# Loading wk and wv as joint 2560-byte rows, taking block 0 four tokens to a partition, and weaving k of the first tiles between the weight folds

## The chip, the cores and the metric

One core of one Trainium2 chip. The time is the device time of one execution in microseconds (us), the median of the undisturbed ("fast") executions. A profile is one execution on the chip; its span is about 1.9 us shorter than the time of the same execution (304.7 against 306.63 us for the kernel before). Times are compared inside the same rounds on the same chip, because the kernel before itself had medians from 306.7 to 307.4 us on different sets of rounds.

## The reference

```python
def A(x, wqkv, w_phi, wo):                      # S = 2048, D = 640, H = 32 heads of Dh = 20
    q, k, v = split(x @ wqkv)
    pq, pk = einsum("hsd,hdf->hsf", q, w_phi), einsum("hsd,hdf->hsf", k, w_phi)
    phi = lambda p: concat([softmax(p, -1), softmax(-p, -1)], -1)
    kv, z = einsum("hsf,hsd->hfd", phi(pk), v), phi(pk).sum(over s)
    o = einsum("hqf,hfd->hqd", phi(pq), kv) / (einsum("hqf,hf->hq", phi(pq), z) + 1e-6)
    return o @ wo
def B(x, w_gate, w_up, w_down):                 # F = 1728
    return (gelu(x @ w_gate) * (x @ w_up)) @ w_down
g = sigmoid((x * gate_w).sum(-1))
out = g * A(x) + (1 - g) * B(x)                 # all in bf16
```

## The kernel before

The 2048 tokens are 16 tiles of 128. Before the steady state, the kernel has a start-up of some 28 us, and only that is touched here:

1. `xtok` (the first four tiles of x) is transposed by TensorE (PE), two tiles copied by ScalarE (ACT), two by VectorE (DVE).
2. v of the four tiles is computed, contraction slab by slab, as the slabs of wv arrive.
3. wk is transposed by PE (six head groups) and multiplied by a block-diagonal matrix of w_phi: the "fold". The five folded slabs `wk2` give k already mapped through w_phi. The same is done with wq, whose transposes come from six transposing loads (`wqT`).
4. k of the tiles 0 to 3, exp of k on ACT (`Ek`), then the q projections (`pq`), and from there on a stream of v/k, q and Gram products (`gram`: v times the normalised exps of k; `k_norm`: DVE normalises them).

`self.ps`, the memory that PE writes its products to, is divided by this program into eight banks of 512 columns. A product that overwrites a bank has to wait until ACT or DVE has read out what stood there.

```python
# loads (order of issue)
xload(0, "sp"); xload(2, "act"); xload(1, "sp"); xload(3, "act")     # 160 KB each, rows of 1280 bytes
for kt in range(KD):                                                  # five slabs of wv, 160 KB each
    sc.dma("sp", ... self.wvk[:, kt, 0:D] <- w3[:, kt, 2 * D:3 * D], writes=[("wv", kt)])
sc.dma("act", ... wphi_sb <- w_phi)                                   # rows of 40 bytes
sc.dma("sp", ... self.wk_raw <- w3[:, :, D:2 * D], writes=["wk_raw"]) # 800 KB
sc.dma("sp", gload, writes=["wgate"])                                 # gate_w as a column, 2-byte elements
for g in range(6):                                                    # six transposing loads of wq
    sc.dma("sp", ... dma_start_transpose(self.wqT[:, g, :], ...), reads=["wk_raw"] if g == 0 else [])
... three transposing loads of x (tiles 4 to 15), then all FFN weights ...

# attention_state, start-up
for i in range(NWARM): matmul on zeros into bank 3                    # 7, warm-up
for t, ek in enumerate("adad"): self.x_transpose(t, 4 + t, ek)
self.v_first({... wk transposes of two groups inside the last slab ...})
self.w_transposes("k", (2, 3, 4, 5), (0, 6, 7, 0), "dadd")
...
for kt, (bk, ek) in enumerate(zip((6, 1, 4, 6, 0), "adada")):         # a: copied by ACT, d: by DVE
    self.fold(kt, "k", (bk, bk + 1), ek)
self.k_early(0, 2)            # k of tile 0 in the PSUM banks 2, 3; then its exp on ACT
self.k_early(1, 4)
self.fold(0, "q", (6, 7), "d")
self.fold(1, "q", (0, 1), "a")
self.k_early(2, 2)
self.fold(2, "q", (6, 7), "d")
self.fold(3, "q", (0, 1), "a")
self.fold(4, "q", (6, 7), "d")
self.k_norm(0)
self.k_early(3, 4)
self.k_norm(1)
self.pq(0, 1, 1); self.pq(0, 0, 0); self.pq(0, 3, 3)
self.gram(0)
self.k_norm(2)
self.pq(0, 2, 2)
...
```

The softmax here doesn't subtract the row's maximum and nothing guards it: scores larger than these inputs give would overflow.

## Time and profile before

| | before |
|---|---|
| time, median of the first 4 executions | 306.72 us (306.5 to 307.06) |
| span of the profile | 304.7 us |
| PE busy | 298.0 us |
| first v product / first q projection / third q projection | 6.93 / 25.46 / 28.12 us |

The page of the kernel before, its first and its busy line, and the first line of the chain that ended last:

```profile
span 304.7 us, 5022 instructions
PE 298.0 (98%) x2011; PEld 175.3 (58%) x2011; DVE 160.0 (53%) x312; ACT 106.8 (35%) x189; POOL 29.8 (10%) x59
PE 94%; DMA 2%; ACT 1%; DVE 1%; issue 0%; SPq 0%; ACTq 0%; DVEq 0%
```

PE is the bottleneck over the whole span. What is left to win is the time in which PE stands still. The table of stretches of the kernel before shows where most of that is (columns: stretch in us from the span's start and its length, then busy us of PE, weight loads, DVE, ACT, POOL with instruction counts, PE's granted clock, DMA share, GB/s):

```profile
4.00:8.00 4.00, 3.38 (x30) 2.58 (x28) 0.98 (x2) 1.41 (x2) 3.13 (x21) 1.00 1.01 302
...
16.00:20.00 4.00, 3.51 (x36) 2.31 (x34) 1.65 (x2) 2.65 (x6) 0.00 (x0) 1.00 0.69 129
20.00:24.00 4.00, 3.32 (x44) 2.71 (x42) 1.65 (x2) 3.99 (x10) 0.00 (x0) 1.00 0.91 190
24.00:28.00 4.00, 3.79 (x26) 1.95 (x23) 3.56 (x5) 2.85 (x7) 0.00 (x0) 1.00 1.11 224
```

0.62 us are lost from 4 to 8 us, 0.49 from 16 to 20, 0.68 from 20 to 24, 0.21 from 24 to 28. The view of waits, for PE alone, names what ended each idle time (total us, times, longest; left out are the wait for the first operand, at 1.26 us, and a later one of 0.2 us):

```profile
PE ps L345 <- DVE wq_50 L358: 0.7, 1, 0.7
PE ps L376 <- DMA wvk<-in_A_wqkv_dram: 0.6, 1, 0.6
PE ps L488 <- ACT Eq L494: 0.3, 1, 0.3
PE ps L345 <- ACT wvk L360: 0.3, 1, 0.3
PE ps L365 <- DVE wvk L358: 0.2, 1, 0.2
```

L376 is v, L345 the folds, L365 k, L488 the q projections. The timeline of the kernel before (start us, duration us, engine, line, out<-in, count, idle time before and what ended it) has the steps:

```profile
6.93 2.34 PE L376 MATMUL ps<-wvk,xT 128*128 128x480 bf16 x16 [0.62 <-DMA wvk<-in_A_wqkv_dram]
...
10.63 8.33 SPq L227 DMA_TRANSPOSE wqT<-in_A_wqkv_dram  x6
...
19.29 1.30 ACT L423 ACTIVATE Ek<-ps 128x640 bf16<-128x640 f32 x2 [1.04 <-PE ps L365]
...
20.39 0.77 PE L345 MATMUL ps<-BD,wqT 120*128 120x120 bf16 x12
...
21.00 1.53 PE L365 MATMUL ps<-wvk,xT 128*128 128x384 bf16 x10
...
25.46 2.32 PE L488 MATMUL ps<-xT,wq_50 128*128 128x512 bf16 x10
```

They are: v; the issue of the six wq transposes, which waits for wk; exp of k of tile 0; the first wq folds; k of tile 2 ("third k"); the first two q projections. Two marks are read from the chain of waits of the kernel before: the last product of the first wk fold, which waits for a copy of the transposed wk (the piece of the chain that starts there takes in three products of the next fold), and the third q projection, behind which PE never waits again for more than 0.2 us:

```profile
15.53 0.37 PE ps L345 x4
...
28.12 1.25 PE ps L488 x5
```

### The profile page before, as it was taken

The page shows a single profiled execution, that of the slowest core. Times are in us where ns is not written, and L with a number is a line of the kernel's source. Part 1 is how long each engine was busy: PE and PEld are TensorE (multiplying, and loading weights), DVE is VectorE, ACT ScalarE, POOL GpSimd, SP SyncE. Part 2 cuts the span into 40 slices and gives each one's busy share as a digit, 9 for nine tenths or more (in the row PEclk, how much of TensorE's full clock was granted, in tenths as well). Part 3 has the DMA queues.
Part 4 walks back from the last instruction along what each step waited for, and adds up shares of the span by engine and source line. Part 5 has one row for each costly group of instructions (what it writes and reads, how often), then busy time and mean ns, then how long its engine had stood idle before and what let it go on. Part 6 is the DMA issues. An engine that isn't in the chain of part 4 may idle for free.

```text
span 304.7 us, 5022 instructions
## 1 busy us (share of the span) xinstructions
PE 298.0 (98%) x2011; PEld 175.3 (58%) x2011; DVE 160.0 (53%) x312; ACT 106.8 (35%) x189; POOL 29.8 (10%) x59
## 2 busy tenths in 40 slices
PE   7998999999999999999999999999999999999996
PEld 4664565655555555677545567754457764545763
DVE  1438999586775877234367710435770044567000
ACT  3388666667674222111322211123221122222111
POOL 7100000000000011111011000101110010111000
PEclk9999999999999999999999999999999999999999
DMA  7589996000000011120120111011111001110401
GB/s 222 140 150 209 369 369 221 0 2 0 2 0 0 2 22 24 24 65 25 43 20 4 22 24 43 24 43 23 17 6 44 24 26 41 22 22 0 45 22 45
DMA packets 34641, 18.29 MB, mean 60 GB/s; under 512 B 25850, under 2 KB 34618, under 8 KB 34618
## 3 DMA queue, kind: packets, MB, share of 16 engines
q1 hardware_dynamic: 33680, 17.62, 22.8%
q10 hardware_dynamic: 938, 0.35, 0.4%
q8 instruction: 16, 0.26, 0.4%
q14 instruction: 7, 0.06, 0.1%
HBM read 9.78 MB, written 2.62 MB: 41 GB/s over the span
## 4 chain that ended last, share of the span: by engine, by line
PE 94%; DMA 2%; ACT 1%; DVE 1%; issue 0%; SPq 0%; ACTq 0%; DVEq 0%
PE ps L572 37%; PE ps L654 20%; PE ps L365 12%; PE ps L660 7%; PE ps L488 6%; PE ps L609 4%; PE ps L462 4%; PE ps L376 2%; DMA wvk<-in_A_wqkv_dram 2%; PE ps L582 1%; PE ps L345 1%; ACT Eq L494 1%; PE ps L327 0%; ACT Ek L423 0%; DVE wkT L334 0%
## 5 line engine op out<-in xcount | busy, mean ns | idle before, releaser
L572 PE MATMUL ps<-xT,wu_sb 128*128 128x512 bf16 x260 | 64.6, 379 | 0.2 <-ACT Eq L494 0.2
L572 PE MATMUL ps<-xT,wg_sb 128*128 128x512 bf16 x260 | 64.6, 379 | 0.0
L654 PE MATMUL ps<-wd_sb,hT 128*128 128x320 bf16 (+2 forms) x448 | 63.8, 299 | 0.0
L575 ACT ACTIVATE gl<-ps 128x512 bf16<-128x512 f32 x52 | 31.1, 597 | 83.2 <-PE ps L572 81.0
L577 DVE TENSOR_TENSOR hT<-ps,gl 128x512 bf16<-128x512 f32 x52 | 35.7, 688 | 42.9 <-PE ps L572 42.9
L654 PEld LDWEIGHTS ps<-wd_sb,hT 128*128 128x128 bf16 x448 | 43.1, 98 | 18.2 <-DVE hT L577 0.4
L572 PEld LDWEIGHTS ps<-xT,wu_sb 128*128 128x128 bf16 x260 | 25.4, 98 | 31.1 <-issue 0.7
L365 PE MATMUL ps<-wvk,xT 128*128 128x512 bf16 (+2 forms) x220 | 40.6, 335 | 0.2 <-DVE wvk L358 0.2
L572 PEld LDWEIGHTS ps<-xT,wg_sb 128*128 128x128 bf16 x260 | 24.9, 98 | 26.9
L670 ACT ACTIVATE outsb<-ps,Gm 128x640 bf16<-128x640 f32 (+2 forms) x17 | 13.0, 763 | 74.1 <-PE ps L660 74.1
L638 POOL TENSOR_TENSOR Og<-O_59,O_60 128x640 bf16<-128x640 bf16 x16 | 22.3, 1396 | 167.8 <-DVE O_60 L636 167.8
L365 PEld LDWEIGHTS ps<-wvk,xT 128*128 128x128 bf16 x220 | 21.1, 97 | 19.5 <-DVE wvk L358 0.6
L434 DVE TENSOR_REDUCE Dk<-Ek 128x64 f32<-128x1280 bf16 x16 | 23.7, 1482 | 10.0 <-ACT gcol L426 10.0
L625 DVE RECIPROCAL RH<-ps 128x32 f32<-128x32 f32 x16 | 5.7, 358 | 43.9 <-PE ps L609 42.8
L443 DVE TENSOR_TENSOR Ek<-Ek,Dk 128x640 bf16<-128x640 bf16 x32 | 25.0, 822 | 0.5
L488 PE MATMUL ps<-xT,wq_50 128*128 128x512 bf16 x100 | 24.7, 378 | 0.3 <-ACT Eq L494 0.3
L660 PE MATMUL ps<-wo_sb,goT 128*128 128x320 bf16 (+2 forms) x160 | 24.5, 299 | 0.0
L494 ACT ACTIVATE Eq<-ps 128x512 bf16<-128x512 f32 x40 | 21.8, 607 | 5.4 <-PE ps L488 5.4
L423 ACT ACTIVATE Ek<-ps 128x640 bf16<-128x640 f32 x32 | 20.7, 703 | 2.2 <-PE ps L365 2.2
L660 PEld LDWEIGHTS ps<-wo_sb,goT 128*128 128x128 bf16 x160 | 15.5, 98 | 6.3
L609 PEld LDWEIGHTS ps<-KV,Eq 128*128 128x128 bf16 x192 | 12.0, 98 | 3.1
L609 PE MATMUL ps<-KV,Eq 128*128 128x154 bf16 x192 | 13.7, 221 | 0.0
(68 smaller groups left out, 178.7 us busy)
## 6 DMA issues: line engine op xcount, KB each, us to landing
out_dram<-outsb SPq DMA_DIRECT2D x15, 160.0 KB, 1.8
wd_sb<-in_B_w_down_dram SPq DMA_DIRECT2D x1, 2080.0 KB, 12.7
wg_sb<-in_B_w_gate_dram SPq DMA_DIRECT2D x1, 1120.0 KB, 7.0
wu_sb<-in_B_w_up_dram SPq DMA_DIRECT2D x1, 1120.0 KB, 9.5
wg_sb<-in_B_w_gate_dram SPq DMA_DIRECT2D x1, 960.0 KB, 9.0
wu_sb<-in_B_w_up_dram SPq DMA_DIRECT2D x1, 960.0 KB, 9.4
wvk<-in_A_wqkv_dram SPq DMA_DIRECT2D x5, 160.0 KB, 4.8
wk_raw<-in_A_wqkv_dram SPq DMA_DIRECT2D x1, 800.0 KB, 6.5
```

Source lines behind the costliest of these rows:

```text
L365: sc.op("pe", lambda e, kt=kt: e.matmul(self.bank(bank)[:, bcol:bcol + n], self.xT[:, kt, t * P:(t + 1) * P], self.wvk[:, kt, c0:c0 + n], ...
L434: sc.op("dve", lambda e: e.tensor_reduce(self.Dk[:, se, 0, :].rearrange("p (s h) -> p s h", h=H), self.Ek[:, se, :, :].rearrange("p s (h d ...
L443: sc.op("dve", lambda e, v=v, r=r: e.tensor_tensor(v, v, r, ALU.mult), reads=[("Rk", se)], writes=[("Ek", se, s)])
L488: sc.op("pe", lambda e, kt=kt: e.matmul(self.bank(bank), self.wq2[:, kt, i * P:(i + 1) * P], self.xT[:, kt, b * self.BT:(b + 1) * self.BT] ...
L494: sc.op("act", lambda e, s=s, scale=scale: e.activation(self.Eq[:, s, i, b * self.BT:(b + 1) * self.BT], self.bank(bank), AF.Exp, scale=sc ...
L572: sc.op("pe", lambda e, kt=kt, w=w, bk=bk: e.matmul(self.bank(bk), w[:, kt, c * P:(c + 1) * P], xs(kt), start=(kt == 0), stop=(kt == self. ...
L575: sc.op("act", lambda e: e.activation(self.gl[:, slot, :], self.bank(banks[0]), AF.Gelu_apprx_tanh), reads=[("ps", banks[0])], writes=[("g ...
L577: sc.op("dve", lambda e: e.tensor_tensor(self.hT[:, c, :], self.bank(banks[1]), self.gl[:, slot, :], ALU.mult), reads=[("ps", banks[1]), ( ...
L609: sc.op("pe", lambda e, s=s, i=i, n=n, o0=o0, k0=k0, bk=bk, r=r: e.matmul(self.bank(bk)[:, o0:o0 + n], self.Eq[:, s, i, t * P:(t + 1) * P] ...
L638: sc.op("pool", lambda e: e.tensor_tensor(self.Og[:, sl, :], self.O1[:, sl, :], self.O2[:, sl, :], ALU.add), reads=[("O", 0, sl), ("O", 1, ...
L654: sc.op("pe", lambda e: e.matmul(self.bank(bk, w), self.hT[:, c, tt * P:(tt + 1) * P], self.wd_sb[:, c, w0:w0 + w], start=(c == 0), stop=F ...
L660: sc.op("pe", lambda e: e.matmul(self.bank(bk, w), self.goT[:, gs, k, :], self.wo_sb[:, k, w0:w0 + w], start=False, stop=(k == self.KD - 1 ...
```

## The change

Its intent: wk and wv are neighbours in a row of wqkv, so one row of both is a run of 2560 bytes instead of two of 1280. x gets the same run length when a partition holds four consecutive tokens (tokens 4p to 4p+3) instead of one token of each tile; the outputs of block 0 are then stored with the same token order. The gate column is built by five tiny PE products from a row of gate_w. The x transposes, v and the wk transposes are woven together so that PE can start as slabs land. From the first fold on, k of tiles 0 and 1 is computed slab by slab right behind each folded slab ("k behind the fold") instead of after all five folds. Sums keep their operands; only tokens of block 0 trade places inside the block.

```diff
-        xload(0, "sp")
-        xload(2, "act")
-        xload(1, "sp")
-        xload(3, "act")
-        for kt in range(KD):
-            sc.dma("sp", ... self.wvk[:, kt, 0:D] <- w3[:, kt, 2 * D:3 * D] ..., writes=[("wv", kt)])
+        x4 = self.x[0:self.BT, :].rearrange("(p j) n -> p j n", j=self.TB)
+        def xload(j):
+            sc.dma("sp", ... self.xtok[:, j:j + 2, :] <- x4[:, j:j + 2, :] ..., writes=[("xtok", j), ("xtok", j + 1)])
+        def kvload(kt):
+            sc.dma("sp", ... self.w3[:, kt, 0:2 * D] <- w3[:, kt, D:3 * D] ..., writes=[("wv", kt), ("wk", kt)])
         sc.dma("act", ... wphi_sb <- w_phi ...)
-        sc.dma("sp", ... self.wk_raw <- w3[:, :, D:2 * D] ..., writes=["wk_raw"])
-        (gate_w as a column by DMA; wqT transposes wait for wk_raw)
+        sc.dma("act", ... self.gw_row <- gate_w ...)
+        xload(0); kvload(0); xload(2); kvload(1) ... kvload(4)
+        (wqT transposes wait for ("wk", 4))
 [...]
+        warm(7)
+        xt(0, 6, "a"); xt(1, 7, "d")
+        warm(2)
+        vs(0, 0); self.gate_column(3); vs(1, 0)
+        xt(2, 6, "a"); xt(3, 7, "d")
+        vs(0, 1); vs(1, 1); vs(2, 0); vs(3, 0); vs(2, 1); vs(3, 1)
+        self.blockdiag((6, 7))
+        ... v of slabs 2, 3; then the six wk transposes between the v products of slab 4 ...
-        for kt, (bk, ek) in enumerate(zip((6, 1, 4, 6, 0), "adada")):
-            self.fold(kt, "k", (bk, bk + 1), ek)
-        self.k_early(0, 2)
-        self.k_early(1, 4)
+        self.fold(0, "k", (6, 7), "d")
+        self.fold(1, "k", (4, 5), "a")
+        ks(0, 0); ks(1, 0)                        # k of tiles 0, 1 with slab 0, in banks 0,1 and 2,3
+        self.fold(2, "k", (6, 7), "d")
+        ks(0, 1); ks(1, 1)
+        self.fold(3, "k", (4, 5), "a")
+        self.fold(4, "k", (6, 7), "d")
+        ks(0, 2); ks(1, 2); ks(0, 3); ks(1, 3)
+        ks(0, 4); self.k_evac(0, 0)               # exp of tile 0
+        ks(1, 4); self.k_evac(1, 2)               # exp of tile 1
         self.fold(0, "q", (6, 7), "d")
-        self.fold(1, "q", (0, 1), "a")
-        self.k_early(2, 2)
+        self.fold(1, "q", (4, 5), "d")
+        self.k_early(2, 0)
         self.fold(2, "q", (6, 7), "d")
-        self.fold(3, "q", (0, 1), "a")
-        self.fold(4, "q", (6, 7), "d")
+        self.fold(3, "q", (4, 5), "d")
+        self.fold(4, "q", (6, 7), "a")
         self.k_norm(0)
-        self.k_early(3, 4)
+        self.k_early(3, 2)
 [...]
+            if t < self.TB:                       # stores of block 0 in the new token order
+                rows = self.out[0:self.BT, :].rearrange("(p j) n -> p j n", j=self.TB)[:, t, :]
```

More of the change, by code (lines that the diff above doesn't have):

```diff
@@ L157, in alloc @@
         self.zero = T("zero", [P, 512], BF16)
+        self.gw_row = T("gw_row", [1, D], BF16)
+        self.one = T("one", [1, 1], BF16)
         self.gcol = T("gcol", [P, NT], F32)
@@ L186, in alloc @@
         place([
-            [("wvk", [P, KD, 2 * D + 2], BF16), ("wq2", [P, KD, D], BF16)],
+            [("w3", [P, KD, 3 * D + 2], BF16), ("wq2", [P, KD, D], BF16)],
             [("hT", [P, NFC, BT], BF16), ("gl", [P, 3, BT], BF16)],
@@ L190, in alloc @@
         place([
-            [("xtok", [P, self.TB, D], BF16), ("wk_raw", [P, KD, D], BF16),
-             ("wkT", [P, 6, D], BF16), ("wqT", [P, 6, D], BF16), ("wq_raw", [P, KD, D], BF16)],
+            [("xtok", [P, self.TB, D], BF16), ("wkT", [P, 6, D], BF16), ("wqT", [P, 6, D], BF16)],
             [("goT", [P, 6, KD, P], BF16), ("O1", [P, 2, D], BF16), ("O2", [P, 2, D], BF16),
@@ L208, in loads @@
         w3 = self.wqkv.rearrange("(kt p) n -> p kt n", p=P)
-        def gload(e):
-            with nc.allow_non_contiguous_dma(reason="gate_w as a column"):
-                return e.dma_start(self.wvk[:, :, 2 * D:2 * D + 1], self.gw.rearrange("(kt p o) -> p kt o", p=P, o=1))
-        def xload(t, q):
-            sc.dma(q, lambda e: e.dma_start(self.xtok[:, t, :], self.x[t * P:(t + 1) * P, :]), writes=[("xtok", t)])
-        xload(0, "sp")
-        xload(2, "act")
-        xload(1, "sp")
-        xload(3, "act")
@@ L219, in loads @@
-        for kt in range(KD):
-            sc.dma("sp", lambda e, kt=kt: e.dma_start(self.wvk[:, kt, 0:D], w3[:, kt, 2 * D:3 * D]), writes=[("wv", kt)])
+        x4 = self.x[0:self.BT, :].rearrange("(p j) n -> p j n", j=self.TB)
+        def xload(j):
+            sc.dma("sp", lambda e: e.dma_start(self.xtok[:, j:j + 2, :], x4[:, j:j + 2, :]),
+                   writes=[("xtok", j), ("xtok", j + 1)])
+        def kvload(kt):
+            sc.dma("sp", lambda e: e.dma_start(self.w3[:, kt, 0:2 * D], w3[:, kt, D:3 * D]), writes=[("wv", kt), ("wk", kt)])
@@ L221, in loads @@
         sc.dma("act", lambda e: e.dma_start(self.wphi_sb[:, :].rearrange("d (h f) -> d h f", f=DH),
                                             self.wphi.rearrange("h d f -> d h f")), writes=["wphi"])
-        sc.dma("sp", lambda e: e.dma_start(self.wk_raw[:, :, :], w3[:, :, D:2 * D]), writes=["wk_raw"])
-        if self.QDMA:
-            sc.dma("sp", gload, writes=["wgate"])
-            for g, (h0, nh) in enumerate(self.GH):
-                sc.dma("sp", lambda e, g=g, h0=h0: e.dma_start_transpose(
-                    self.wqT[:, g, :], self.wqkv[:, h0 * DH:h0 * DH + P]),
-                    reads=["wk_raw"] if g == 0 else [], writes=[("wqT", g)])
-        else:
-            sc.dma("sp", lambda e: e.dma_start(self.wq_raw[:, :, :], w3[:, :, 0:D]), writes=["wq_raw"])
-            sc.dma("sp", gload, writes=["wgate"])
+        sc.dma("act", lambda e: e.dma_start(self.gw_row[0:1, :], self.gw.rearrange("(o n) -> o n", o=1)), writes=["gw_row"])
@@ L234, in xblock @@
+        xload(0)
+        kvload(0)
+        xload(2)
+        for kt in range(1, KD):
+            kvload(kt)
+        for g, (h0, nh) in enumerate(self.GH):
+            sc.dma("sp", lambda e, g=g, h0=h0: e.dma_start_transpose(
+                self.wqT[:, g, :], self.wqkv[:, h0 * DH:h0 * DH + P]),
+                reads=[("wk", KD - 1)] if g == 0 else [], writes=[("wqT", g)])
         def xblock(b, after=()):
@@ L237, in xblock @@
                 reads=after, writes=[("xT", t) for t in range(b * 4, b * 4 + 4)])
-        xblock(1, [] if self.QDMA else ["wq_raw"])
+        xblock(1)
         xblock(2)
@@ L317, in blockdiag, with wk_transposes @@
             reads=rd, writes=["BD"])
-    def w_transposes(self, which, gs, banks, ekeys):
+    def wk_transposes(self, gs, banks, ekeys):
         sc = self.sc
-        raw, T = (self.wk_raw, self.wkT) if which == "k" else (self.wq_raw, self.wqT)
         for g, b, ek in zip(gs, banks, ekeys):
@@ L327, in w_transposes, with gate_column @@
                 sc.op("pe", lambda e, kt=kt: e.transpose(
-                    pv[0:rows, kt * P:(kt + 1) * P], raw[:, kt, h0 * self.DH:h0 * self.DH + rows], self.ident[:, :]),
-                    reads=["w%s_raw" % which, "ident"], writes=[("ps", b)], signal=(kt == self.KD - 1))
-            dst = T[0:rows, g, :]
+                    pv[0:rows, kt * P:(kt + 1) * P], self.w3[:, kt, h0 * self.DH:h0 * self.DH + rows],
+                    self.ident[:, :]),
+                    reads=[("wk", kt), "ident"], writes=[("ps", b)], signal=(kt == self.KD - 1))
+            dst = self.wkT[0:rows, g, :]
             src = pv[0:rows, 0:self.D]
-            wr = [("w%sT" % which, g)]
             if ek == "d":
-                sc.op("dve", lambda e: e.tensor_copy(dst, src), reads=[("ps", b)], writes=wr)
+                sc.op("dve", lambda e: e.tensor_copy(dst, src), reads=[("ps", b)], writes=[("wkT", g)])
             else:
-                sc.op("act", lambda e: e.activation(dst, src, AF.Copy), reads=[("ps", b)], writes=wr)
+                sc.op("act", lambda e: e.activation(dst, src, AF.Copy), reads=[("ps", b)], writes=[("wkT", g)])
+    def gate_column(self, b):
+        sc = self.sc
+        for kt in range(self.KD):
+            sc.op("pe", lambda e, kt=kt: e.matmul(
+                self.bank(b)[:, kt:kt + 1], self.gw_row[0:1, kt * P:(kt + 1) * P], self.one[0:1, 0:1],
+                start=(kt == 0), stop=(kt == self.KD - 1), skip_group_check=True),
+                reads=["gw_row", "one"], writes=[("ps", b)], signal=(kt == self.KD - 1))
+        sc.op("dve", lambda e: e.tensor_copy(
+            self.w3[:, :, 3 * self.D:3 * self.D + 1], self.bank(b, self.KD).unsqueeze(2)),
+            reads=[("ps", b)], writes=["wgate"])
     def fold(self, kt, which, banks, ekey):
@@ L350, in fold @@
         if which == "k":
-            dst = self.wvk[:, kt, self.D:2 * self.D]
+            dst = self.w3[:, kt, 2 * self.D:3 * self.D]
         else:
@@ L365, in proj @@
             sc.op("pe", lambda e, kt=kt: e.matmul(
-                self.bank(bank)[:, bcol:bcol + n], self.xT[:, kt, t * P:(t + 1) * P], self.wvk[:, kt, c0:c0 + n],
+                self.bank(bank)[:, bcol:bcol + n], self.xT[:, kt, t * P:(t + 1) * P], self.w3[:, kt, self.D + c0:self.D + c0 + n],
                 start=(kt == 0), stop=(kt == self.KD - 1)),
@@ L369, in proj, with v_step, k_step @@
                 writes=[("ps", bank)], signal=(kt == self.KD - 1))
-    def v_first(self, extra):
+    def v_step(self, t, kt):
         sc = self.sc
-        for kt in range(self.KD):
-            for t in range(4):
-                for c0, n, bk, col in ((0, 480, t, 0), (480, 160, 4 + t // 3, 160 * (t % 3))):
-                    sc.op("pe", lambda e, kt=kt, t=t, c0=c0, n=n, bk=bk, col=col: e.matmul(
-                        self.bank(bk)[:, col:col + n], self.xT[:, kt, t * P:(t + 1) * P], self.wvk[:, kt, c0:c0 + n],
-                        start=(kt == 0 and col == 0), stop=(kt == self.KD - 1), skip_group_check=True),
-                        reads=[("xT", t), ("wv", kt)], writes=[("ps", bk)], signal=(kt == self.KD - 1))
-                for f in extra.get((kt, t), ()):
-                    f()
+        for c0, n, bk, col in ((0, 480, t, 0), (480, 160, 4 + t // 3, 160 * (t % 3))):
+            sc.op("pe", lambda e, c0=c0, n=n, bk=bk, col=col: e.matmul(
+                self.bank(bk)[:, col:col + n], self.xT[:, kt, t * P:(t + 1) * P], self.w3[:, kt, self.D + c0:self.D + c0 + n],
+                start=(kt == 0 and col == 0), stop=(kt == self.KD - 1), skip_group_check=True),
+                reads=[("xT", t), ("wv", kt)], writes=[("ps", bk)], signal=(kt == self.KD - 1))
+    def k_step(self, t, kt):
+        sc = self.sc
+        for c0, n, bk, col in ((640, 384, 2 * t, 128), (1024, 257, 2 * t + 1, 0)):
+            sc.op("pe", lambda e, c0=c0, n=n, bk=bk, col=col: e.matmul(
+                self.bank(bk)[:, col:col + n], self.xT[:, kt, t * P:(t + 1) * P], self.w3[:, kt, self.D + c0:self.D + c0 + n],
+                start=(kt == 0), stop=(kt == self.KD - 1)),
+                reads=[("xT", t), ("wk2", kt), "wgate"], writes=[("ps", bk)], signal=(kt == self.KD - 1))
     def v_first_evac(self, ts, ek, tail):
@@ L510, in attention_state @@
         order = [(b, i) for b in range(self.NB) for i in range(self.KD)]
-        self.sc.op("dve", lambda e: e.memset(self.zero[:, :], 0.0), writes=["zero"])
-        for i in range(self.NWARM):
-            self.sc.op("pe", lambda e: e.matmul(self.bank(3), self.zero[:, 0:P], self.zero[:, :], start=True, stop=True),
-                       reads=["zero"], writes=[("ps", 3)])
-        for t, ek in enumerate("adad"):
-            self.x_transpose(t, 4 + t, ek)
-        tk = lambda g, b, ek: (lambda: self.w_transposes("k", (g,), (b,), ek))
@@ L518, in attention_state @@
-        ve = lambda ts, ek, tail=False: (lambda: self.v_first_evac(ts, ek, tail))
-        self.v_first({(1, 3): [lambda: self.blockdiag((6, 7))],
-                      (4, 0): [ve([0], "a")],
-                      (4, 1): [tk(0, 6, "d"), ve([1], "a")],
-                      (4, 2): [tk(1, 7, "d"), ve([2], "a")]})
-        self.w_transposes("k", (2, 3, 4, 5), (0, 6, 7, 0), "dadd")
-        ve([0, 1, 2], "a", True)()
-        ve([3], "a")()
-        ve([3], "a", True)()
-        for kt, (bk, ek) in enumerate(zip((6, 1, 4, 6, 0), "adada")):
-            self.fold(kt, "k", (bk, bk + 1), ek)
@@ L529, in attention_state, with warm @@
-        self.k_early(0, 2)
-        self.k_early(1, 4)
+        sc = self.sc
+        sc.op("dve", lambda e: e.memset(self.zero[:, :], 0.0), writes=["zero"])
+        sc.op("dve", lambda e: e.memset(self.one[:, :], 1.0), writes=["one"])
+        def warm(n):
+            for i in range(n):
+                sc.op("pe", lambda e: e.matmul(self.bank(3), self.zero[:, 0:P], self.zero[:, :], start=True, stop=True),
+                      reads=["zero"], writes=[("ps", 3)])
+        vs, ve, xt = self.v_step, self.v_first_evac, self.x_transpose
@@ new lines, in attention_state @@
+        tk = lambda g, b, ek: self.wk_transposes((g,), (b,), ek)
+        warm(7)
+        xt(0, 6, "a")
+        xt(1, 7, "d")
+        warm(2)
+        vs(0, 0)
+        self.gate_column(3)
+        vs(1, 0)
+        xt(2, 6, "a")
+        xt(3, 7, "d")
+        vs(0, 1)
+        vs(1, 1)
+        vs(2, 0)
+        vs(3, 0)
+        vs(2, 1)
+        vs(3, 1)
+        self.blockdiag((6, 7))
+        for kt in (2, 3):
+            for t in range(4):
+                vs(t, kt)
+        tk(0, 6, "d")
@@ new lines, in attention_state @@
+        tk(1, 7, "a")
+        vs(0, 4)
+        ve([0], "a", False)
+        vs(1, 4)
+        tk(2, 6, "d")
+        ve([1], "a", False)
+        vs(2, 4)
+        tk(3, 7, "d")
+        ve([2], "a", False)
+        vs(3, 4)
+        tk(4, 0, "d")
+        tk(5, 1, "d")
+        ve([0, 1, 2], "a", True)
+        ve([3], "a", False)
+        ve([3], "a", True)
+        ks = self.k_step
+        self.fold(0, "k", (6, 7), "d")
+        self.fold(1, "k", (4, 5), "a")
+        for t in (0, 1):
+            ks(t, 0)
@@ L531, in attention_state @@
+        self.fold(2, "k", (6, 7), "d")
+        for t in (0, 1):
+            ks(t, 1)
+        self.fold(3, "k", (4, 5), "a")
+        self.fold(4, "k", (6, 7), "d")
+        for kt in (2, 3):
+            for t in (0, 1):
+                ks(t, kt)
+        for t in (0, 1):
+            ks(t, 4)
+            self.k_evac(t, 2 * t)
         self.fold(0, "q", (6, 7), "d")
-        self.fold(1, "q", (0, 1), "a")
-        self.k_early(2, 2)
+        self.fold(1, "q", (4, 5), "d")
+        self.k_early(2, 0)
@@ L595, in num @@
         DB, DH = self.DB, self.DH
-        old = [("xtok", k) for k in range(4)] + ["wk_raw"] + [("wkT", g) for g in range(6)] + [("wqT", g) for g in range(6)] + ["wq_raw"]
+        old = [("xtok", k) for k in range(4)] + [("wkT", g) for g in range(6)] + [("wqT", g) for g in range(6)]
         parts = {0: [(0, 0, 6), (1, 6, 12), (2, 12, 15)], 1: [(2, 16, 19), (3, 19, 25), (4, 25, 31)]}
@@ L671, in evac @@
                   reads=[("ps", k) for k in bks] + ["Gm"], writes=[("outsb", os_, w)for w in ((0, 320) if n == 640 else (w0,))])
-            sc.dma("sp", lambda e: e.dma_start(self.out[t * P:(t + 1) * P, w0:w0 + n], self.outsb[:, os_, w0:w0 + n]),
+            rows = self.out[t * P:(t + 1) * P, :]
+            if t < self.TB:
+                rows = self.out[0:self.BT, :].rearrange("(p j) n -> p j n", j=self.TB)[:, t, :]
+            sc.dma("sp", lambda e: e.dma_start(rows[:, w0:w0 + n], self.outsb[:, os_, w0:w0 + n]),
                    reads=[("outsb", os_, w) for w in ((0, 320) if n == 640 else (w0,))], writes=[("out", t, w0)])
@@ L686 @@
     NUMB = 2
-    NWARM = 7
-    QDMA = True
-    oldw = [(w, k) for w in ("wv", "wk2", "wq2") for k in range(5)] + ["wgate"]
+    oldw = [(w, k) for w in ("wk", "wv", "wk2", "wq2") for k in range(5)] + ["wgate"]
     def ffn(self):
```

## The prediction

> **What bounds it now.** TensorE. The page has PE busy 298.0 of 304.7 us. In the chain of waits PE holds 94%. In the stretches table PE is idle 2.6 us after 4 us, nearly all of it before 28 us. The change touches only what precedes the first projection of q (25.46 us in the timeline): idle 0.62 us before the first v matmul (waiting for wv, landed at 6.8), some 1.5 us around the folds of wk (15.0 to 18.1), 0.97 us in the folds of wq (22.83 to 23.80, on a DVE copy), 0.5 us at 27.6.
>
> **Loads.** Same bytes. Four x loads of 160 KB (landed 3.1 to 3.6 us after issue), five wv loads of 160 KB (4.7 to 5.1) and wk of 800 KB (6.5, complete 10.6 us) become two and five of 320 KB in 2560-byte runs. From 2.5 to 9 us the 16 engines are already full (share about 1.0, 224 to 392 GB/s). I estimate wk+wv complete at about 10, first wk/wv slab at 5.5 to 6. wphi now goes first and shares the engines with the first x load: the Trainium skill (DMA: Bandwidth & Descriptors, "Issuing engines are not separate DMA queues") says both queues run on the same 16 engines.
>
> **PE up to the folds.** Removed: the 0.62 us wait. Added: two warm matmuls (0.43 us each while cold) and five tiny gate matmuls (about 0.06 each). Cheaper: half of the x transposes move past the warm-up. The 20 transposes now take 2.09 us, wk's 5 take 0.28 us: clock 1 : 2; the Trainium skill (TensorE: Matmul & The Clock Gate, "What's actually happening") puts the switch after about 3.4 us of sustained work, and here it is seen at about 5.9 us. These cancel. The wk transposes are spread among v, so their copies (DVE 0.49, ACT 0.70 us) no longer line up: I put the end of the first fold at 15.6 to 15.8, now 15.90.
>
> **PE from the folds on.** New order: fold, two tiles' k step, fold. DVE takes folds 0, 2, 4 (0.83 us each), so the last k step cannot start before about 20.2; k of both ends at about 20.7 (now 20.55). But both tiles end together: exp of k (two of 0.65 us on ACT, 1.30) starts at about 20.7, now 19.29. The third k then takes bank 0, free at about 22.1, while PE has only 1.0 us of work: a new wait near 0.5 us. The q folds wait about 0.7 us for DVE copies, as now. First q projection: about 26 to 26.6, now 25.46; the wait for ACT before the third q projection stays, 0.5 to 0.7.
>
> **Sum.** First fold -0.2; k +0.3; new bank wait +0.5; ACT later +0.2: about +0.8 by hand. I discount that for slack I do not see: +0.35.
>
> Predicted 307.0 us, 8 in 10 from 304.8 to 308.4. Chances: faster by over 2% 0.02, within 2% 0.96, slower by over 2% 0.02.
>
> **Right if:** PE's idle before v gone; wk+wv landed by 10 us; first wk fold done near 15.7; PE waiting about 0.5 us for ACT exp before the third k; q projections starting at 26 or later.
>
> **Wrong if:** the 2560-byte runs move much faster, so v starts at once and first fold ends before 15.3 (then 305); wphi in front delays the first x load past 4.6 us (then slower by as much); or the spread wk transposes let the k chain end before 20, which brings the q projections forward (then 305 to 306).

## The result, and the profile after

| | before | after |
|---|---|---|
| median of 4 executions each | 306.72 us (306.5 to 307.06) | 307.64 us (307.11 to 308.09) |
| ratio of fast runs | | 1.0028, 95% interval 1.0006 to 1.0051 |
| six more executions, other rounds | 307.25 us (11 runs) | 307.59 us, ratio 1.0010, 0.9997 to 1.0022 |
| span of the profile | 304.7 us | 305.3 us |

A ratio is the mean time of one kernel's fast runs over that of the other's of the same rounds, so it is not quite the ratio of the medians quoted. The change is within 2%, and if anything it loses a few tenths of a us.

The page after: the span, the busy line and the chain by engine.

```profile
span 305.3 us, 5031 instructions
PE 298.3 (98%) x2018; PEld 174.6 (57%) x2018; DVE 161.6 (53%) x316; ACT 105.6 (35%) x187; POOL 29.8 (10%) x59
PE 95%; ACT 2%; DVE 1%; issue 1%; ACTq 0%; DVEq 0%
```

The DMA that held 2% of the chain is gone from it, and ACT's share went from 1% to 2% (both rounded). The stretches after, same columns:

```profile
4.00:8.00 4.00, 3.91 (x39) 2.15 (x38) 1.17 (x3) 1.41 (x2) 3.15 (x22) 1.00 1.01 376
...
16.00:20.00 4.00, 3.50 (x36) 2.51 (x37) 1.95 (x3) 1.39 (x2) 0.00 (x0) 1.00 0.68 129
20.00:24.00 4.00, 3.21 (x38) 2.43 (x36) 1.93 (x3) 3.29 (x8) 0.00 (x0) 1.00 1.15 244
24.00:28.00 4.00, 3.49 (x25) 2.15 (x26) 3.93 (x6) 2.96 (x8) 0.00 (x0) 1.00 1.10 215
```

From 4 to 8 us PE gained 0.53 us and the DMA moved 376 instead of 302 GB/s. From 20 to 28 us PE lost 0.41 us; from 16 to 20 its busy time is the same. PE's waits after, with the same ones left out, and one of 0.2 us for a copy of the transposed wk:

```profile
PE ps L353 <- DVE wq_50 L366: 0.7, 1, 0.7
PE ps L373 <- ACT gcol L438: 0.6, 1, 0.6
PE ps L390 <- DVE w_49 L366: 0.5, 1, 0.5
PE ps L500 <- ACT Eq L506: 0.3, 1, 0.3
```

The wait for wv is gone, and so are the two waits for copies of folded wk (0.3 and 0.2 us). Two are new: L390 (the k steps woven between the folds) waits 0.5 us for the DVE copy of the first folded slab, and L373 (the third k) waits 0.6 us for ACT to have read bank 0. The timeline after, the lines that answer to those of before:

```profile
5.62 0.45 PE L382 MATMUL ps<-w_49,xT 128*128 128x480 bf16 x2
...
9.40 8.41 SPq L228 DMA_TRANSPOSE wqT<-in_A_wqkv_dram  x6
...
16.36 0.72 PE L390 MATMUL ps<-w_49,xT 128*128 128x384 bf16 x4 [0.47 <-DVE w_49 L366]
...
20.34 1.30 ACT L435 ACTIVATE Ek<-ps 128x640 bf16<-128x640 f32 x2 [1.34 <-PE ps L390]
20.36 0.74 PE L353 MATMUL ps<-BD,wqT 120*128 120x120 bf16 x12
...
21.70 1.54 PE L373 MATMUL ps<-w_49,xT 128*128 128x384 bf16 x10 [0.60 <-ACT gcol L438]
...
26.18 2.32 PE L500 MATMUL ps<-xT,wq_50 128*128 128x512 bf16 x10
```

And the two marks in the chain of waits after:

```profile
15.16 0.22 PE ps L353
...
28.83 1.25 PE ps L500 x5
```

v starts 1.3 us earlier, the wq transposes are issued 1.2 us earlier, and yet the first wk fold ends only 0.37 us earlier. From there to the third q projection it takes 28.83 - 15.16 = 13.67 us instead of 28.12 - 15.53 = 12.59. From the third q projection to the end both need 276.5 to 276.6 us (305.3 - 28.83 and 304.7 - 28.12). So the whole difference lies before 29 us, and the question has two halves: what did the new front really bring, and why is the stretch from the first fold to the q projections 1.1 us longer?

**Theory A.** The new order from the first fold on costs about 1.2 us: both tiles' k end together, so ACT's exp starts late and bank 0, which the third k needs, comes free late. The new front brings somewhat less than that.
**Rival B.** The front (loads, clock, gate products, token order of the stores) brings nothing or costs, and the waits seen further down are only where the delay shows.

### The profile page after: what moved, and what is told of

It is laid out like the page before. It is cut to its first block, busy times and chain, and to the rows that moved or that the text cites. A ratio compares the mean times of both kernels' runs of the same rounds, so it can differ in the third digit from the quotient of the medians.

```text
span 305.3 us, 5031 instructions
## 1 busy us (share of the span) xinstructions
PE 298.3 (98%) x2018; PEld 174.6 (57%) x2018; DVE 161.6 (53%) x316; ACT 105.6 (35%) x187; POOL 29.8 (10%) x59
## 4 chain that ended last, share of the span: by engine, by line
PE 95%; ACT 2%; DVE 1%; issue 1%; ACTq 0%; DVEq 0%
PE ps L625 36%; PE ps L707 20%; PE ps L373 12%; PE ps L713 7%; PE ps L500 6%; PE ps L662 4%; PE ps L474 4%; PE ps L382 2%; PE ps L635 1%; PE ps L529 1%; ACT Ek L435 1%; PE ps L390 1%; PE ps L353 1%; DVE w_49 L366 1%; ACT Eq L506 1%
## 5 line engine op out<-in xcount | busy, mean ns | idle before, releaser
L373 PE MATMUL ps<-w_49,xT 128*128 128x512 bf16 (+2 forms) x200 | 37.5, 339 | 0.6 <-ACT gcol L438 0.6
L373 PEld LDWEIGHTS ps<-w_49,xT 128*128 128x128 bf16 x200 | 19.3, 97 | 19.1 <-ACT Ek L435 0.7
```

What stands on the lines that cost most here:

```text
L373: sc.op("pe", lambda e, kt=kt: e.matmul(self.bank(bank)[:, bcol:bcol + n], self.xT[:, kt, t * P:(t + 1) * P], self.w3[:, kt, self.D + c0:s ...
```

## The experiments

Twelve runs were made, of ten different kernels (the kernels before and after among them), in three calls, each call on one chip, each run in five rounds beside the kernel before. All were correct. To read them all by one rule, I take from each trace F, the start of the last product of the first wk fold (15.53 us before, 15.15 after), and count from there:

| kernel | clock doubles at | v starts | wq transposes issued | F | first q fold minus F | third k minus F | span minus F | ratio of times to before, 95% interval |
|---|---|---|---|---|---|---|---|---|
| before | 5.9 | 6.93 | 10.63 | 15.53 | 4.86 | 5.47 | 289.17 | 1 |
| b0_again (before) | 6.2 | 6.30 | 10.83 | 14.97 | 4.85 | 6.22 | 289.91 | 1.0005 (0.9991 to 1.0019) |
| e2_newk | 5.2 | 6.72 | 10.99 | 15.32 | 5.21 | 6.81 | 290.52 | 0.9999 (0.9983 to 1.0014) |
| after | before 4.4 | 5.62 | 9.40 | 15.15 | 5.21 | 6.55 | 290.16 | 1.0028 (1.0006 to 1.0051) |
| e0_again (after) | 5.8 | 6.04 | 9.41 | 15.55 | 5.20 | 6.54 | 290.15 | 1.0010 (0.9997 to 1.0022) |
| e3_bank | 6.7 | 6.33 | 9.70 | 16.16 | 5.20 | 5.50 | 289.83 | 1.0005 (0.9988 to 1.0022) |
| e8_newqlate | 5.8 | 6.07 | 9.81 | 15.59 | 5.20 | 6.54 | 289.58 | 0.9999 (0.9987 to 1.0011) |
| e1_oldk | 5.6 | 6.18 | 9.95 | 15.72 | 4.76 | 5.34 | 288.96 | 0.9972 (0.9960 to 0.9985) |
| e1_same | 6.1 | 6.24 | 9.46 | 15.76 | 4.76 | 5.34 | 288.94 | 0.9969 (0.9957 to 0.9981) |
| e4_split | 5.8 | 6.09 | 9.90 | 15.61 | 4.76 | 5.34 | 288.87 | 0.9985 (0.9971 to 0.9999) |
| e6_late | before 4.4 | 5.68 | 11.06 | 15.26 | 4.77 | 5.95 | 289.60 | 0.9997 (0.9985 to 1.0010) |
| e5_qlate | 5.0 | 5.90 | 9.43 | 15.43 | 4.77 | 5.35 | 288.48 | 0.9972 (0.9958 to 0.9985) |
| e5_same | 4.8 | 5.80 | 9.87 | 15.43 | 4.76 | 5.34 | 288.48 | 0.9956 (0.9944 to 0.9968) |
| e7_more | before 4.6 | 5.66 | 9.74 | 15.32 | 4.49 | 5.69 | 288.82 | 0.9941 (0.9929 to 0.9952) |

"Clock doubles" is read from the early products: their distance from start to start halves there (x transposes 107 ns, then 56 ns; products of 512 columns 427 ns, then 213). Where the first transposes already ran at the short distance, it doubled before them; for e3_bank 6.7 is the earliest that fits. The granted clock in the stretches (the column of 1.00) does not show this step.

### e0_again: the changed kernel once more

No edit.

> The changed kernel once more, unchanged, to narrow its ratio and to get a second trace: its four times lay in two groups (307.1 to 307.3 and 308.0 to 308.1), and its x transposes already ran at the doubled clock at 4.6 us, where the kernel before doubled at about 5.9. If the moment of the doubling differs from run to run, this trace shows another moment; a ratio of 1.002 to 1.004 is expected in either case.

307.59 us, ratio 1.0010: a little below what was expected, but overlapping. The second trace doubles its clock at 5.8 instead of before 4.4 us, and F moves from 15.15 to 15.55. From F on both traces of the changed kernel agree to 0.01 us (290.16 and 290.15). So in these two the start varies, and what follows F does not. (In the kernel before it does: 289.17 and 289.91, see b0_again.)

### e1_oldk and e1_same: the new front with the order of the kernel before from the folds on

```diff
-        (fold 0, fold 1, k steps of slab 0, fold 2, ... as in the change, third k in banks 0,1)
+        for kt, (bk, ek) in enumerate(zip((6, 1, 4, 6, 0), "adada")):
+            self.fold(kt, "k", (bk, bk + 1), ek)
+        self.k_early(0, 2); self.k_early(1, 4)
+        (q folds and the third and fourth k as in the kernel before)
```

> The changed kernel with the loads, x transposes, v and wk transposes of the change, but from the first wk fold on the order and banks of the kernel before (five folds, then k of tile 0, then of tile 1, then q folds). Theory A (the new order from the folds on gives away more than the front gains): the front's 0.5 us stays, exp of k starts near 18.8 instead of 20.3, the third q projection near 27.6 instead of 28.8, time about 1.0 to 1.3 us below the changed kernel, so 306.2 to 306.6. Rival B (the loss comes from the new front or from the stores of block 0): the time stays at 307.3 to 308.

> The new front with the old order, again, on one chip with the next three. 306.3 to 306.7, ratio to before 0.997 to 0.9985. Its trace shows no wait of PE for wqT, and from the last product of the first wk fold to the third q projection 12.47 us as in its first trace.

306.35 us against 307.59 of the changed kernel on the same chip: 1.24 us less, as theory A expected and rival B did not. The second time 306.46 us, ratio 0.9969, no wait for wqT, and 12.47 us from F to the third q projection, all as expected. The timeline of e1_oldk:

```profile
15.72 0.79 PE L353 MATMUL ps<-BD,wkT 80*128 80x80 bf16 x13 [0.17 <-DVE wkT L331]
...
16.78 0.75 PE L353 MATMUL ps<-BD,wkT 120*128 120x120 bf16 x12 [0.28 <-ACT w L368]
...
18.23 2.41 PE L373 MATMUL ps<-w,xT 128*128 128x384 bf16 x17 [0.21 <-DVE w L366]
...
19.38 1.30 ACT L435 ACTIVATE Ek<-ps 128x640 bf16<-128x640 f32 x2 [1.05 <-PE ps L373]
20.48 0.74 PE L353 MATMUL ps<-BD,wqT 120*128 120x120 bf16 x12
...
21.06 1.53 PE L373 MATMUL ps<-w,xT 128*128 128x384 bf16 x10
```

exp of k starts 3.66 us after F (after: 20.34 - 15.16 = 5.18), and the third k follows the first q folds without a wait. In numbers: the span after F is 288.95 us with the old order and 290.15 with the new one, a difference of 1.20 us. It divides into two parts. The first q fold starts 4.76 us after F instead of 5.20, which is 0.44 us. No single wait accounts for these: the new order's k steps wait 0.47 us for the copy of the first folded slab, but the old order has waits of 0.28 and 0.21 us in the same stretch, so what makes up the 0.44 us is not shown. The third k starts 0.58 us after the first q fold instead of 1.34, which is 0.76 us (of which 0.60 is PE standing still for ACT). The absolute times of my expectation (exp at 18.8, third q projection at 27.6) were missed; this trace has the latest first x load of all (4.67 us), and its clock doubled later than in the trace after (5.6 against before 4.4 us). The differences held.

### e2_newk: the front of the kernel before with the new order behind it

```diff
-        (five folds, k of tile 0, k of tile 1, q folds as in the kernel before)
+        (fold, k steps of two tiles, fold, ... , banks and q folds as in the change)
```

> The kernel before with only the new order and banks from the first wk fold on (the front unchanged). Theory A: all of the loss without the gain, third q projection at about 29.3, 307.7 to 308.1. Rival B: no slower than before, 306.5 to 307.

This missed: 307.29 us, ratio 0.9999. Theory A expected it half a us to one us slower, and it was not slower: here the time agrees with what rival B expected ("no slower than before"). The timeline of e2_newk shows why:

```profile
21.79 0.50 PE L345 MATMUL ps<-BD,wqT 80*128 80x80 bf16 x7 [0.84 <-DMA wqT<-in_A_wqkv_dram]
22.13 1.53 PE L365 MATMUL ps<-wvk,xT 128*128 128x384 bf16 x10
```

With the old loads, wk lands late, the wq transposes are issued only at 10.99 us, and PE waits 0.84 us for the last of them. While PE waits for wqT, ACT finishes exp of tile 0 and bank 0 comes free; the third k then starts 0.34 us after the wait, with no wait for ACT. So the loss of the new order can hide behind the late wqT; the next run supports this with a comparison. It also means that front and order do not simply add up: with the old front the new order costs nothing that the times show (0.9999).

### b0_again: the kernel before once more

No edit.

> The kernel before once more, unchanged, for a second trace of it: its times on the last chip spread from 306.7 to 308.1, more than the 306.5 to 307.1 of its first runs. Ratio 1.000 within 0.2%. If the spread comes from the last wq transpose landing late (as seen with the before front and the new order, where PE waited 0.84 us for it), a slow execution shows PE waiting for wqT before the first q fold; if it comes from the front, a slow execution shows v starting later than 6.93 us.

Ratio 1.0005, as it should be. Its timeline shows the wait that the first trace of the same kernel had not shown:

```profile
20.85 0.50 PE L345 MATMUL ps<-BD,wqT 80*128 80x80 bf16 x7 [0.61 <-DMA wqT<-in_A_wqkv_dram]
...
28.31 1.25 PE L488 MATMUL ps<-xT,wq 128*128 128x512 bf16 x5 [0.34 <-ACT Eq L494]
```

Here v started (6.30) 0.63 us earlier than in the first trace and F came at 14.97, and PE then gave the lead back waiting 0.61 us for wqT: the third q projection starts at 28.31, not earlier than the 28.12 of the first trace. So the kernel before has two late transfers in a row, wv and wqT, and being early for the first only means waiting for the second. From the arrival of wqT to the third q projection the two orders take the same: 28.31 - 20.85 = 7.46 us here, and 29.26 - 21.79 = 7.47 in e2_newk (its chain of waits has the third q projection at 29.26). The expectation that slow executions show this wait isn't shown: both traced executions of this kernel were among its faster ones (306.63 and 306.83 us).

### e3_bank: the third k in other banks

```diff
         self.fold(0, "q", (6, 7), "d")
-        self.fold(1, "q", (4, 5), "d")
-        self.k_early(2, 0)
-        self.fold(2, "q", (6, 7), "d")
-        self.fold(3, "q", (4, 5), "d")
-        self.fold(4, "q", (6, 7), "a")
+        self.k_early(2, 4)
+        self.fold(1, "q", (6, 7), "d")
+        self.fold(2, "q", (0, 1), "d")
+        self.fold(3, "q", (6, 7), "d")
+        self.fold(4, "q", (0, 1), "a")
```

> The changed kernel with the third k moved to the banks 4 and 5 (one q fold before it instead of two), so that it need not wait until exp of tile 0 has left bank 0. If the 0.6 us wait for that bank is a separate cost: third k starts near 20.7 instead of 21.7 and the time falls by 0.5 to 0.8 us. If only the late exp matters (ACT as the limit before the q projections): the third q projection hardly moves and the time falls by less than 0.3 us.

By time it is inconclusive: 307.25 against 307.59 us of the changed kernel on the same chip, 0.34 us, which lies between the two expectations, and the intervals overlap. Its trace had the latest doubling of the clock of all (6.7 us), so F is at 16.16, and only the count from F can be used. The wait for bank 0 is gone and the third k starts 5.50 us after F instead of 6.54. But of this 1.04 us only 0.32 reach the end (289.83 against 290.15), because the q folds wait for DVE copies:

```profile
24.46 0.46 PE L353 MATMUL ps<-BD,wqT 120*128 120x120 bf16 x6 [0.70 <-DVE wq L366]
25.19 0.46 PE L353 MATMUL ps<-BD,wqT 120*128 120x120 bf16 x6 [0.27 <-DVE wq L366]
```

The first of these waits (0.70 us) the changed kernel has too; the second (0.27) is new, and with it 0.60 - 0.27 = 0.33 us are left of the gain. The bank wait is real, but behind it stands the next limit.

### e6_late: the wq transposes held back

The kernel of e1_oldk, with an idle transfer between the wk/wv slabs and the wq transposes (its bytes are overwritten later by wo).

```diff
+        sc.dma("sp", ... self.wo_sb[:, 0:3, :] <- w3[:, 0:3, D:2 * D] ..., writes=["wo"])
         for g, (h0, nh) in enumerate(self.GH):
-                reads=[("wk", KD - 1)] if g == 0 else [], writes=[("wqT", g)])
+                reads=[("wk", KD - 1), "wo"] if g == 0 else [], writes=[("wqT", g)])
```

> The new front with the old order, and an idle transfer of 480 KB put between the wk/wv slabs and the wq transposes, so that these start about 1.2 us later, at 10.9 to 11.2, as in the kernel before. Theory (the wq transposes have no slack in the kernel before, and their earlier start is a part of the gain): PE waits about 0.7 to 1.2 us for the last one before the first q folds, and the time rises by 0.6 to 1.2 us. If they have slack: less than 0.2 us.

306.98 us, ratio 0.9997: most of the lead over the kernel before is gone. Against e4_split on the same chip it is 0.39 us slower, against the two runs of the kernel it was made from, by ratios of other rounds, 0.8 us (0.9997 against 0.9972 and 0.9969, of 307.2 us). In its trace the span after F is 0.65 us longer (289.60 against 288.95). The wait is there, smaller than expected:

```profile
20.88 0.50 PE L354 MATMUL ps<-BD,wqT 80*128 80x80 bf16 x7 [0.43 <-DMA wqT<-in_A_wqkv_dram]
```

So the early wq transposes are a part of what the new front brings. The idle transfer adds traffic as well, and this run cannot separate the two.

### e4_split: the same loads in runs of 1280 bytes

The kernel of e1_oldk, each slab as two loads.

```diff
-            sc.dma("sp", ... self.w3[:, kt, 0:2 * D] <- w3[:, kt, D:3 * D] ..., writes=[("wv", kt), ("wk", kt)])
+            sc.dma("sp", ... self.w3[:, kt, D:2 * D] <- w3[:, kt, 2 * D:3 * D] ..., writes=[("wv", kt)])
+            sc.dma("sp", ... self.w3[:, kt, 0:D] <- w3[:, kt, D:2 * D] ..., writes=[("wk", kt)])
```

> The new front with the old order behind it (the previous run that was fastest), but each slab of wk and wv loaded as two transfers of 1280-byte runs instead of one of 2560. If the run length matters: the wq transposes start at about 10.4 instead of 9.95 us or later and the time rises by 0.2 to 0.8 us (v or the wk transposes wait for their slab, or wqT comes late). If only the order of the loads matters: no change within 0.2 us.

Inconclusive. 306.59 us, ratio 0.9985, where the joint runs had 0.9972 and 0.9969 in other rounds; the intervals overlap. The stretches from 5 to 8 us show the rate (352 to 375 GB/s here, 382 to 402 in e1_oldk), but the wq transposes were issued at 9.90 us, between the 9.46 and 9.95 of the joint runs, no wait of PE for a slab reached 0.2 us, and from F on the trace is the same within 0.1 us. So the rate is some 9% higher with the joint loads. Those are half as many transfers of twice the size as well as longer runs, and this run changes both at once; no run shows that more than a few tenths of a us of time come of either.

### e5_qlate and e5_same: the last q fold behind the fourth k

The kernel of e1_oldk, two statements moved:

```diff
-        self.fold(4, "q", (6, 7), "d")
-        self.k_norm(0)
         self.k_early(3, 4)
+        self.fold(4, "q", (0, 1), "d")
+        self.k_norm(0)
 [...]
-        self.gram(0)
         self.k_norm(2)
         self.pq(0, 2, 2)
+        self.gram(0)
```

> The new front with the old order, and in it the last q fold moved behind the fourth k (into banks 0 and 1), and the first gram behind the fourth q projection. Theory: the waits between k and the q projections are waits for copies and for ACT's exps, which PE can cover by work it has; the wait of 0.65 us for the DVE copy goes, the third q projection starts near 27.2 instead of 28.2 and the time falls by 0.6 to 1.1 us against the same kernel without the move. Rival (ACT's exps bind there whatever PE does): less than 0.3 us.

> The same with the last q fold moved behind the fourth k. The earlier trace put the fifth k product group 0.6 us nearer to the first fold than without the move: time 0.4 to 0.7 us below the run before it on this chip. Rival (ACT binds there): within 0.2 us.

305.94 against 306.46 us in the same rounds, -0.52 us; the span after F falls by 0.46 us (288.48 against 288.94). The 95% intervals of the two ratios overlap a little (0.9944 to 0.9968 and 0.9957 to 0.9981), but the spans after F agree in both traces of each kernel (288.48 twice, 288.96 and 288.94). The first call had no run of the kernel without the move beside it; its ratio, 0.9972, is that of e1_oldk in other rounds, so by itself it shows no gain. The expected 0.6 to 1.1 us was too much, the later 0.4 to 0.7 held. The timeline of e5_same shows that the fold's wait for DVE is gone and that PE goes from the fourth k through the fold into the q projections:

```profile
22.77 1.53 PE L373 MATMUL ps<-w,xT 128*128 128x384 bf16 x10
...
24.41 0.46 PE L353 MATMUL ps<-BD,wqT 120*128 120x120 bf16 x6
24.71 5.05 PE L500 MATMUL ps<-xT,wq 128*128 128x512 bf16 x20
```

20 projection products of 128x512 take 5.05 us here, where 10 took 2.32: some 0.4 us are now spent waiting inside them. Counted from F, PE reaches the projections 0.53 us earlier than in e1_same (24.71 - 15.43 = 9.28 against 25.57 - 15.76 = 9.81), and 0.46 us of it reach the end.

### e8_newqlate: the same move in the changed kernel

```diff
-        self.fold(4, "q", (6, 7), "a")
-        self.k_norm(0)
         self.k_early(3, 2)
+        self.fold(4, "q", (4, 5), "d")
+        self.k_norm(0)
         (and gram(0) behind pq(0, 2, 2))
```

> The changed kernel, its order kept for k of tiles 0 and 1 and for the third k, with only the last q fold behind the fourth k and the first gram behind the fourth q projection. Theory: the PE wait of 0.7 us for a DVE copy goes, and the time falls by 0.5 to 1.0 us below the changed kernel, to 306.6 to 307.1, while the late exp and the wait for bank 0 stay, so that it stays 0.5 to 1.1 us above the same move in the old order.

307.29 us, 0.9999 of before, 0.2 us above the expected range. The span after F falls by 0.57 us against the changed kernel (289.58 against 290.15), and it stays 1.10 us above the same move in the old order (288.48); in time 1.35 us above e5_same in the same rounds, somewhat more than expected. Its timeline keeps the wait of the changed kernel:

```profile
22.13 1.54 PE L373 MATMUL ps<-w,xT 128*128 128x384 bf16 x10 [0.60 <-ACT gcol L438]
```

This is the second pair of kernels with the same front and another order (and with it other banks and copying engines), and from F on it gives the same 1.1 to 1.2 us. So with the new front rival B is refuted. With the old front (e2_newk) the order's cost does not show, and with the new order the new front gains nothing: e2_newk had 307.29 us and the changed kernel 307.59 in the same rounds, with overlapping intervals.

### e7_more: two further steps

The kernel of e5_qlate, with x tiles 0 and 2 copied by DVE and 1 and 3 by ACT, and the wk folds in the bank pairs (6,7), (2,3), (4,5), (0,1), (6,7).

```diff
-        xt(0, 6, "a"); xt(1, 7, "d")      # and the same for tiles 2, 3
+        xt(0, 6, "d"); xt(1, 7, "a")
-        for kt, (bk, ek) in enumerate(zip((6, 1, 4, 6, 0), "adada")):
-            self.fold(kt, "k", (bk, bk + 1), ek)
+        for kt, (bks, ek) in enumerate(zip(((6, 7), (2, 3), (4, 5), (0, 1), (6, 7)), "adada")):
+            self.fold(kt, "k", bks, ek)
```

> The same, and besides the copies of x tiles 0 and 2 given to DVE (0.49 us) and of 1 and 3 to ACT (0.70 us), and the wk folds laid in four pairs of banks so that the fourth need not wait for the copy of the first. Theory: v starts 0.2 us earlier where the clock doubles early, and the wait of 0.28 us for an ACT copy inside the folds goes: 0.2 to 0.5 us below the run before it.

305.51 us against 305.94 of e5_same and 307.39 of the kernel before in the same rounds, ratio 0.9941: the fastest kernel, 1.9 us under the kernel before. The wait inside the folds is gone (the first q fold starts 4.49 us after F instead of 4.76). That v starts earlier is not shown (5.66 us, against 5.62 and 5.68 in the other traces whose clock doubled early), and the two steps were not run apart. The execution traced was the slowest of its five (306.09 us) and shows the next limit, wqT again:

```profile
20.67 0.50 PE L353 MATMUL ps<-BD,wqT 80*128 80x80 bf16 x7 [0.45 <-DMA wqT<-in_A_wqkv_dram]
```

## Why the prediction was right or wrong

The range and the class held (307.64 us in 304.8 to 308.4, within 2%), and most of the mechanism did.

- **"First q projection: about 26 to 26.6", "the third k then takes bank 0 ... a new wait near 0.5 us": right.** 26.18 us and a wait of 0.60 us; the second trace, e0_again, has the same wait and 26.79 us, just outside. With e1_oldk and e8_newqlate it is shown that, behind the new front, the order costs this.
- **"k +0.3": right.** From F to the first q fold the k phase took 0.34 us more than in the kernel before (5.20 against 4.86), 0.44 more than in e1_oldk.
- **"ACT later +0.2": not separate.** From the third k to the third q projection both orders take 7.13 us (28.83 - 21.70 after, 28.19 - 21.06 in e1_oldk). The cost lies in the start of the third k: 0.76 us, where 0.5 was put down for its wait. Order altogether: 1.20 us against e1_oldk, 1.08 against the first trace of the kernel before (13.67 - 12.59); 1.0 predicted (0.3 + 0.5 + 0.2).
- **"First fold -0.2": this step is not borne out.** In the first trace after it was -0.37. Over the ten traces with the new front whose first steps are alike (all but e7_more), F averages 15.57 us, over the three with the old front 15.27. That average is not a fair one: the traced executions of e1_oldk and e1_same were the slowest and second slowest of theirs, those of the kernel before fast ones. What holds in every trace is this: the idle time before v did go, as predicted, and v starts earlier (5.62 to 6.33 us against 6.30 to 6.93), but from there to F the new front needs 9.5 to 9.8 us instead of 8.6 to 8.7, and half of the x transposes and the gate products now stand in between (0.72 and 0.27 us in the trace after). And with the new front F follows the moment at which the clock doubles: 15.15 and 15.26 us where it doubled before 4.4, 15.43 at 4.8 and 5.0, 15.55 to 15.61 at 5.8, 15.76 at 6.1, 16.16 at 6.7 (e1_oldk, whose first x load came late, lies off this row with 15.72 at 5.6). The -0.37 came with an early clock; at 5.8 to 5.9 F is 15.55 to 15.61 against 15.53. In place of a gain here, part of the gain came from a step that the prediction left out:
- **Left out: the wq transposes.** The prediction counted wk and wv landing at about 10 us (right: 9.40) and drew nothing from it. In two of the three traces with the old loads PE waits 0.61 and 0.84 us for the last wq transpose, issued behind wk. In the traces of after, e0_again, e1_oldk and e1_same it does not; with the new loads as they are, only the fastest kernel, e7_more, meets this wait again. I had read one trace of the kernel before, in which wv came late and hid this; b0_again shows that once v starts earlier, wqT has no slack.
- **"I discount that for slack I do not see: +0.35": not needed in the first rounds** (+0.86 us by the ratio, the +0.8 by hand), about right in the second (+0.3). The two sets of rounds overlap, so the size is known only as roughly 0 to 0.9 us. That the sum came out right is partly luck: the first fold's gain and the wqT transposes were errors of opposite sign, and the discount stood for neither.
- **"Wrong if wphi in front delays the first x load past 4.6 us":** the first x transposes started at 4.37 to 4.67 us with the new loads and at 4.22 with the old, so this cost is there at 0.15 to 0.45 us. The first x load is also twice as large as before, and no run moved wphi alone, so that it is wphi is only argued.

So the account is: with the old order the new front is worth about 0.9 us (e1_oldk and e1_same against before, ratios 0.9972 and 0.9969), behind it the new order costs 1.2 us, and the sum is a small loss. Taken the other way round, the new order costs nothing with the old front (e2_newk) and the new front put before it brings no gain (307.59 against 307.29 us, intervals overlapping). So the two figures hold for the first of these ways only. What stays open: of the 0.9 us the traces show the wait for wqT (0.61 us in b0_again), and e6_late gives back 0.4 to 0.8 us by delaying wqT, but the slower executions of the kernel before (307.2 to 308.1 us) were never traced, so it is not shown what holds them.

Two places of the skill were used. The Trainium skill (DMA: Bandwidth & Descriptors, "Issuing engines are not separate DMA queues") says that transfers issued by different engines run on the same 16 DMA engines; the traces do not contradict it, since the two x loads, with wphi beside the first, landed 3.9 us after their issue (median), where the four x loads of half the size had landed in 3.1 and 3.4 us (medians of the two queues), but with the size doubled as well no run isolates it. The Trainium skill (TensorE: Matmul & The Clock Gate, "What's actually happening") puts the doubling of the clock after about 3.4 us of sustained work and calls its window free-running; the traces agree that it moves from run to run, but not that 3.4 us come first: in the trace after, the transposes ran at the short distance from 4.44 us at the latest, 3.2 us after PE's first product.

## What to carry to other kernels

When a start-up is bounded by several transfers and copies in a row, a step that comes earlier only shows which later one is next: count from a common mark in the trace, and do it in more than one trace of the same kernel, before calling a transfer free. Interleaving two tiles makes both finish at the late end; if another engine must work on each of them, finish the first one early. Two changes that each take away a wait need not add up, so test each with and without the other. To cover a wait for a copy, move a piece of PE work that does not depend on it into the gap (one moved fold was worth 0.5 us here), and expect the engine behind to give back a part.

## What the Trainium skill lacked or had wrong

- TensorE: Matmul & The Clock Gate, "What's actually happening": it gives the moment of the doubling a variation of ±500 ns, though a note in the same section counts 6, 11 or 14 slow products in runs of one kernel. In the traces here, all with PE at work from 1.26 us (with pauses of at most 0.24 us up to the doubling), the doubling came from before 4.4 us (after, e6_late) to 6.7 us (e3_bank), a spread of over 2.2 us. In the changed kernel the first fold moved from 15.15 to 15.55 us between two executions with the doubling before 4.4 and at 5.8, and over the traces with the new front a later doubling goes, by and large, with a later first fold, so this can be a cause of the spread of its times (307.11 to 308.09 us); that is argued, not tested.
- DMA: Bandwidth & Descriptors: it has no figure for runs of 1280 against 2560 bytes in loads issued by SP. Here, from 5 to 8 us, with the 16 engines full, they moved 352 to 375 GB/s (e4_split) and 382 to 402 GB/s (e1_oldk, in half as many transfers).
- No page that I used says how long a chain of transposing loads takes from its first issue to its last landing; all that was found is a bandwidth. Here six of 160 KB took 8.2 to 9.0 us to issue from SP one after another (8.33 before, 8.97 in e1_same), and the product that waited for the last one started 9.8 us (e6_late), 10.0 (b0_again), 10.8 (e2_newk) and 10.9 us (e7_more) after the first issue. So the time of the first issue sets when the last lands only to about 1 us.
